# RWKV-7 attention with hash-routed experts on one core: the loads of tiles 4 to 7, the third round of decays, the order of transposes and scores, and the turnings

## The chip, the cores and the metric

The kernel runs on one core of one Trainium2 chip. The metric is the time of one execution on the device in microseconds (us); a lower one is better. Several engines work side by side, each through its own queue, strictly in order: TensorE (PE, matmuls and transposes), VectorE (DVE), ScalarE (ACT), GpSimd (POOL) and SyncE (SP, which here only issues transfers). ACT and POOL can issue transfers as well. An instruction that waits holds everything behind it on its engine.

## The reference, cut to what matters

```python
B, H, S, D = (4, 8, 768, 40)          # r, k, v, w, a, b: (B, H, S, D), float32
for t in range(S):
    y[:, :, t] = einsum('bhd,bhde->bhe', r_t, state)
    Sa = einsum('bhde,bhe->bhd', state, a_t)
    state = state * w_t[:, :, None, :] - einsum('bhd,bhe->bhde', Sa, b_t)
    state = state + einsum('bhd,bhe->bhde', v_t, k_t)
x = y.transpose(0, 2, 1, 3).reshape(3072, 320)
expert = token_ids * 2654435761 % 8
for e in range(8):                     # w1[e]: 320 x 1024, w2[e]: 1024 x 320
    out[expert == e] = relu(x[expert == e] @ w1[e]) @ w2[e]
```

The first half is a recurrence over 768 steps with a 40 x 40 state for each of 32 heads; the second half sends each of 3072 tokens through one of eight experts.

## The kernel before, in words

**Tiles.** The recurrence is done in chunks of 64 steps. A tile is one chunk of one of two pairs of batches, so there are 24 tiles; tile u belongs to chunk u // 2. Four tiles (two chunks) share a *round* of decays, so there are six rounds, 0 to 5. Four tiles also share one *inversion* of small triangular blocks on DVE.

**Decays** (`decays`, one call for each round). The decays w are loaded (`pb`), clamped (L270), multiplied up as prefixes and suffixes (L275, L292), and closed by `own` (L280, L282), an `exchange` of block ends on PE (`ex_ps`), `ends` (ACT L297 to L302, DVE L299) and `recip` (L306, L307). `spread_all` multiplies the results through (L311; on GpSimd from round 1 on). Then p and q are turned so that time lies on partitions: by DVE (`turned`, L315), with three copies for the second half of q (L333 to L335, by SP except in round 0); round 1 instead writes both to DRAM and reads them back (`store` L340, L323, L329), all on SP's queue. `t_turn` holds the ticks of `turn_p` and `turn_q`.

**Preparing a tile** (`tile_a`). a goes into `at`, b and k into `z` (a slot of `z_all`; four transfers at L420, each 64 rows of eight runs of 160 bytes). GpSimd (DVE for tiles 0 to 3) multiplies `at` by p and `z` by q (L427). PE transposes them (`t_ps` L490, `z_ps` L458), ACT copies the result out (`at_t` L444, `z_t` or `cv` L459). PE forms the scores `a_ps` (L218, reading `z_t` and `at_t`); ACT copies parts of them out (`no`, `pk`), and `mk` is their masked copy: by DVE (L486), or for tiles 4 to 7 by ACT (L483) and then GpSimd (L484).

**Inversion** (`group_i`). DVE turns `pk` (`nb`, L512), does 31 pairs of products and sums (L521, L524), and turns the result twice (`ut` L532, `ug` L533).

**The recurrence** (`tile_m`, `tile_s`, `tile_b`). It follows the preparation at a distance of eight tiles: `x_ps` and `u_ps` (from `ut`, `ug`), `r_ps` in two parts, `c_ps`, `rc_ps`, whose masked copy is `mr` (DVE L650), `nc_ps`, `s_ps`, whose scaled copy `sc` (DVE L676) is the new state, `y_ps` and its copy `xs` (L694), which GpSimd's queue stores into `x_rows`. The routing of tokens (`routing`) is laid between, a step every half tick; its first step loads the tokens (`tok`, L741) and reads them on DVE (`eid`, L748).

**Order.** Every piece of work is registered with a *tick*; the pieces are sorted by tick and emitted in that order, and this is the order in each engine's queue. Tile u's preparation lies around tick u (closer for tiles 4 to 7), its recurrence around tick u + 8. PSUM buffers for `z_ps`, `t_ps`, `a_ps` and others alternate between two.

**Experts.** After the recurrence, rows of `x_rows` are gathered by expert, go through two matrix products (`up_ps`, `dn_ps`) and are scattered to the output.

Of the kernel before, what the change touches and what calls it, by code (L numbers as in the profile page):

```python
# [18 lines left out]
def kernel(  # L19
# [13 lines left out]
    nc = tc.nc  # L33
# [8 lines left out]
    NG = B // 2  # L42
# [87 lines left out]
    def at_tick(tick, step=None, order=0):  # L130
        if step is not None:
            tick += STEPS.index(step) / len(STEPS)

        def add(f):
            plan.append((round(tick, 4), order, len(plan), f))
            return f
        return add
# [11 lines left out]
    at_r = ring("at", 3, [P, HP, P], gaps, 3)  # L149
    NZ = LAG + 2  # L150
    z_all = hold.tile([P, NZ, 2, HP, P], F32, name="z_all")
    for lo, hi, when in ((0, 4, -9.0), (4, NZ, -3.0)):
        @at_tick(when)
        def _(lo=lo, hi=hi):
            nc.gpsimd.memset(z_all[:, lo:hi].rearrange("p i b hp (two x) -> p (i b hp two) x", two=2)[:, :, D:C], 0.0)

    def z_r(u):
        return z_all[:, u % NZ]
# [17 lines left out]
    for be in range(2):  # L176
        rows = slice(be * C, (be + 1) * C)
# [49 lines left out]
    def per_head(t):  # L227

        return t.rearrange("t hp (two x) -> t (hp two) x", two=2)[:, :, 0:D]
# [156 lines left out]
    def tile_a(u):  # L386

        n, g = divmod(u, NG)
        ri, rn = divmod(n, RN)
        x = tiles[u]  # L390

        early = u < 2 * NG
        second = 2 * NG <= u < 4 * NG
        eng = (nc.sync, nc.scalar)[u % 2] if early else nc.sync
        if early:
            t_in = t_inz = -8.9 + 0.01 * u
            t_mul = -6.0 + 0.01 * u
            t_mulz = -6.1 + 0.01 * u if u < 2 else t_mul - 0.005
            t_z, t_at, t_a = u - 0.3, (-0.15, 0.5, 0.95, 1.0)[u], u + 0.9 if u < 3 else u + 0.4
        elif second:  # L400
            base = 4 + 0.7 * (u - 4)
            t_in = t_inz = (0.55, 0.97, 0.2, 1.05)[u - 4]
            t_mul = base - 0.5
            t_mulz = t_mul
            t_z, t_at, t_a = base - 0.3, base - 0.15, base + 0.4
        else:
            t_in, t_inz, t_mul, t_mulz = u - 2.3, u - 1.42, u - 0.9, u - 0.6
            t_z, t_at, t_a = (u - i + STEPS.index(n) / len(STEPS) for i, n in ((0, "z"), (1, "at_t"), (0, "a")))

        @at_tick(t_in)  # L410
        def _():
            x["z"] = z_r(u)
            x["at"] = r1_r(u // GRP) if u in (3, 7) else at_r(u)
            load(eng, x["at"][:], a, g, n * C)

        @at_tick(t_inz)
        def _():
            for be in range(2):
                for src, rows in ((b, half(be)), (k, half(1 - be))):
                    eng.dma_start(per_head(x["z"][rows, be]),  # L420
                                  src[batch(g, be), :, n * C:(n + 1) * C, :].rearrange("h t e -> t h e"))

        cols = slice((rn * NG + g) * DM, (rn * NG + g + 1) * DM)

        def times(eng, t, by):
            t = per_head(t)
            eng.tensor_tensor(t, t, by.rearrange("p (h e) -> p h e", e=D), op=OP.mult)  # L427

        @at_tick(t_mul)
        def _():  # L430
            times(nc.vector if early else nc.gpsimd, x["at"][:], rounds[ri]["p"][:, cols])

        @at_tick(t_mulz)
        def _():
            for be in range(2):
                times(nc.vector if early else nc.gpsimd, x["z"][:, be], rounds[ri]["q"][:, be, cols])

        @at_tick(t_at)
        def _():
            x["at_t"] = t = at_t_r(u)  # L440
            p = psum("t_ps")
            for be in range(2):
                turn(p, 0, x["at"][half(be)], be, half(be))
            nc.scalar.copy(t[:].rearrange("p b hp t -> p b (hp t)"), p[:, :, 0:HP * C])  # L444

        @at_tick(t_z)
        def _():
            if early and u % 2:
                z_t = cv[:].rearrange("p a b t -> p (a b t)").rearrange("p (b hp i t) -> p b hp i t", b=2, hp=HP, i=2)
            else:  # L450
                z_t = work.tile([P, 2, HP, 2, C], F32, tag="z_t", name="z_t", bufs=1)[:]
            x["z_t"] = z_t
            p = psum("z_ps")
            for i in range(2):
                for be in range(2):
                    for hp in range(HP):
                        c0 = (be * HP + hp) * C
                        nc.tensor.transpose(p[:, i, c0:c0 + C], x["z"][half(i), be, hp, :], ident[half(i), half(i)])  # L458
            nc.scalar.copy(z_t.rearrange("p b hp i t -> p i (b hp) t"), p[:].rearrange("p i (h t) -> p i h t", t=C))  # L459

        @at_tick(t_a)
        def _():
            gi, ti = divmod(u, GRP)
            p = psum("a_ps")
            for kind in range(2):
                for hp, par, be in quarters():
                    i = be ^ kind
                    c0 = (kind * HP + hp) * C
                    mm(p[half(i), par, c0:c0 + C], x["z_t"][half(par), be, hp, i, :], x["at_t"][half(par), be, hp, :])
            if ti == 0:  # L470
                groups[gi]["pk"] = work.tile([P, GRP, 2, HP, BLK], F32, tag="pk", name="pk", bufs=1)
            pk = groups[gi]["pk"][:, ti]
            pb, pa = (p[:, :, kind * HP * C:(kind + 1) * HP * C].rearrange("p two (hp t) -> p two hp t", hp=HP) for kind in range(2))
            x["no"] = no = work.tile([P, 2, HP, BLK], F32, tag="no", name="no", bufs=LAG)
            nc.scalar.copy(no[:], pb[..., BLK:])
            nc.scalar.copy(pk, pb[..., 0:BLK])
            for be in range(2):
                low = slice(be * C + BLK, (be + 1) * C)
                nc.scalar.copy(pk[low], pb[low, :, :, BLK:])
            x["mk"] = mk = work.tile([P, 2, HP, C], F32, tag="mk", name="mk", bufs=LAG)  # L480
            mask = after[:].unsqueeze(1).unsqueeze(1).to_broadcast([P, 2, HP, C])
            if second:
                nc.scalar.copy(mk[:], pa)  # L483
                nc.gpsimd.tensor_tensor(mk[:], mk[:], mask, op=OP.mult)  # L484
            else:
                nc.vector.tensor_tensor(mk[:], pa, mask, op=OP.mult)  # L486
# [82 lines left out]
    def tile_s(u, t0):  # L569

        n, g = divmod(u, NG)
        ri, rn = divmod(n, RN)
        x = tiles[u]

        @at_tick(0.4 + 0.2 * u if u < 2 else t0 - 2.0)
        def _():
            x["r"], x["x"] = r_r(u), x_all[:, u % 3]
            load(nc.sync, x["r"][:], r, g, n * C)
            for be in range(2):
                nc.sync.dma_start(per_head(x["x"][half(1 - be), be]),  # L580
                                  v[batch(g, be), :, n * C:(n + 1) * C, :].rearrange("h t e -> t h e"))

        @at_tick(t0 - 0.3)
        def _():
            x["py"] = py = work.tile([P, DM], F32, tag="py", name="py", bufs=1)
            cols = slice((rn * NG + g) * H, (rn * NG + g + 1) * H)
            nc.gpsimd.dma_start(py[:], p_dram[ri][:, cols].rearrange("t c e -> t (c e)"))

        @at_tick(t0 - 1, "rv")
        def _():  # L590
            x["rt"] = t = work.tile([P, 2, HP, C], F32, tag="rt", name="rt", bufs=1)
            p = psum("t_ps")
            for be in range(2):
                turn(p, 0, x["r"][half(be)], 1 - be, half(be))
            for be in range(2):
                turn(p, HP * C, x["x"][half(1 - be), be], be, half(1 - be))
            nc.scalar.copy(t[:].rearrange("p b hp t -> p b (hp t)"), p[:, :, 0:HP * C])
            nc.scalar.copy(cv[:, :, 2:4].rearrange("p hp b t -> p b hp t"),
                           p[:, :, HP * C:].rearrange("p b (hp t) -> p b hp t", hp=HP))
# [110 lines left out]

    t_a = STEPS.index("a") / len(STEPS)
    decays(0, -9.0, -8.0, (-7.9, -7.6), -7.7, -7.5, -6.9, -7.2, None)
    decays(1, -8.5, 0.1, (0.15, 1.85), 1.88, 2.75, 3.02, 2.85, (3.1, 3.15))
    decays(2, -5.5, 0.45, (0.5, 2.5), 3.38, 3.41, 4.0, 3.5, (6.45, 6.46))
    for ri in range(3, NR):
        t = ri * RN * NG
        decays(ri, t - 5.8, t - 5.3, (t - 5.2, t - 3.9), t - 3.75, t - 3.17, t - 2.17, t - 3.1, (t - 1.57, t - 1.44))
    for u in range(NU):
        tile_a(u)
        tile_s(u, u + LAG)  # L720
# [370 lines left out]
```

## Time and profile before

Three timed runs gave 754.02, 762.84 and 766.64 us, median 762.84. The profile comes from a separate execution.

| what | value |
|---|---|
| profiled execution, time | 748.57 us |
| its span (first to last instruction) | 746.8 us |
| mean granted TensorE clock | 0.892 |
| busy: PE, DVE, ACT, POOL | 622.0, 354.7, 272.1, 242.4 us |
| PE busy in 0 to 100 us | 34.1 us |
| PE busy in 140 to 460 us | 300.5 us |
| tile 0's recurrence starts on PE (its first `x_ps`) | 101.39 us |
| transfers | 76.74 MB, mean 103 GB/s |

In the rows below, a time on the left is the start in us from the beginning of the span, and the next number is how long it took. "x16" means 16 instructions merged into one row. "[0.71 <-ACT at_t L444]" says that the engine was idle for 0.71 us before this and what ended the wait. SPq is SP's queue, issuing a transfer. The page's strips cut the span into 40 slices and give the busy share, or the granted clock, in tenths.

### The profile page before, as it was taken

Reading aid. Unit: us, or ns where it says so; the run is one execution under the profiler, and the core shown is the slowest. Engines: PE = TensorE matmul, PEld = TensorE weight load, DVE = VectorE, ACT = ScalarE, POOL = GpSimd, SP = SyncE. Lnnn points to the kernel's source line nnn. Section 1 sums busy time; section 2 is a strip of 40 time slices with the busy share of each in tenths; the row PEclk is TensorE's granted clock in tenths of the full one; section 3 lists DMA queues with packets and bytes.
Section 4 is the critical chain, followed back from the end, with each engine's and each line's share of the span. In section 5 each row is a group of like instructions: output and inputs, shape, how many; then the busy total and the mean of one; then the engine's idle time right before and its main releaser. Section 6 shows DMA issues by size and latency. Waiting matters only on the chain.

```text
span 746.8 us, 24358 instructions
## 1 busy us (share of the span) xinstructions
PE 622.0 (83%) x10686; PEld 467.0 (63%) x10686; DVE 354.7 (47%) x721; ACT 272.1 (36%) x611; POOL 242.4 (32%) x311
## 2 busy tenths in 40 slices
PE   0450588999899989999998994498999999999994
PEld 0340577888787777878887884255556465565652
DVE  6889564897866768576495211115311111102100
ACT  1550454467556646756754461111010101111010
POOL 4060754525473664453321011503022121310101
PEclk9995556599789989999998898599899999999997
DMA  9479253356647644663343223967413253120000
GB/s 164 104 114 183 46 117 61 60 116 142 110 69 152 103 73 106 129 112 57 53 61 62 50 57 117 354 223 252 146 43 92 93 182 101 52 89 9 27 3 29
DMA packets 164158, 76.74 MB, mean 103 GB/s; under 512 B 143247, under 2 KB 155536, under 8 KB 164049
## 3 DMA queue, kind: packets, MB, share of 16 engines
q1 hardware_dynamic: 151632, 57.76, 35.5%
q0 software_dynamic: 5952, 16.08, 7.1%
q10 hardware_dynamic: 6464, 1.31, 1.1%
q8 instruction: 85, 1.39, 0.8%
q14 instruction: 25, 0.20, 0.1%
HBM read 58.69 MB, written 12.82 MB: 96 GB/s over the span
## 4 chain that ended last, share of the span: by engine, by line
PE 48%; issue 19%; DVE 12%; ACT 7%; POOL 5%; DMA 4%; SPq 3%; POOLq 0%; DVEq 0%; ACTq 0%
PE dn_ps L926 7%; PE up_ps L906 5%; PE r_ps L218 5%; PE rc_ps L218 4%; PE s_ps L218 4%; PE u_ps L218 3%; PE t_ps L490 3%; PE y_ps L218 3%; PE a_ps L218 3%; POOL xg L885 3%; PE z_ps L458 2%; PE c_ps L218 2%; PE sd_ps L706 2%; PE nc_ps L659 2%; PE up_ps L902 2%
## 5 line engine op out<-in xcount | busy, mean ns | idle before, releaser
L926 PE MATMUL dn_ps<-w,ht 128*128 128x320 f32 x384 | 104.9, 433 | 0.0
L906 PE MATMUL up_ps<-xt,w 128*128 128x416 f32 x256 | 97.6, 536 | 0.0
L926 PEld LDWEIGHTS dn_ps<-w,ht 128*128 128x128 f32 x384 | 72.8, 190 | 32.1 <-issue 1.9
L916 POOL DMA_INDIRECT out_dram<-o,idx_all x26 | 25.7, 989 | 194.5 <-ACT o L915 187.4
L697 POOL DMA_DIRECT2D x_rows<-xs x48 | 26.8, 562 | 163.8 <-DVE xs L694 120.5
L906 PEld LDWEIGHTS up_ps<-xt,w 128*128 128x128 f32 x256 | 49.2, 197 | 48.4 <-issue 48.4
L524 DVE TENSOR_TENSOR ub<-ub,outer 128x31 f32<-128x31 f32 (+15 forms) x186 | 65.0, 349 | 6.4
L521 DVE TENSOR_TENSOR outer<-ub,nb 128x31 f32<-128x31 f32 (+15 forms) x186 | 63.0, 339 | 7.4 <-ACT ub L506 2.8
L909 DVE TENSOR_SCALAR ht<-up_ps 128x416 f32<-128x416 f32 x32 | 18.9, 592 | 98.8 <-PE up_ps L906 98.8
L891 DVE COPY xt<-xg_ps 128x384 f32<-128x384 f32 x24 | 12.1, 552 | 101.8 <-PE xg_ps L890 101.8
L458 PE MATMUL z_ps<-ident,z_all 64*128 64x64 f32 x384 | 31.2, 270 | 34.8 <-POOL z_all L427 24.6
L650 DVE TENSOR_TENSOR mr<-rc_ps,after 128x1024 f32<-128x1024 f32 x24 | 29.3, 1222 | 60.3 <-PE rc_ps L218 60.3
L458 PEld LDWEIGHTS z_ps<-ident,z_all 64*128 64x128 f32 x384 | 27.0, 174 | 37.6 <-POOL z_all L427 25.6
L915 ACT COPY o<-dn_ps 128x320 f32<-128x320 f32 x24 | 10.2, 425 | 101.6 <-PE dn_ps L926 101.6
L427 POOL TENSOR_TENSOR z_all<-z_all,qt 128x320 f32<-128x320 f32 x40 | 33.9, 864 | 33.9 <-DMA z_all<-in_k_dram 14.7
L911 ACT ACTIVATE ht<-up_ps 128x416 f32<-128x416 f32 x32 | 16.0, 515 | 68.1 <-PE up_ps L906 68.1
L218 PE MATMUL rc_ps<-rt,cv 64*64 64x64 f32 x1536 | 37.0, 240 | 3.9 <-issue 2.5
L679 ACT COPY st<-sc 40x320 f32<-40x320 f32 x44 | 20.1, 457 | 55.1 <-DVE sc L676 54.9
L902 PE MATMUL up_ps<-xt,w 64*128 64x416 f32 x128 | 30.8, 568 | 8.0 <-DVE xt L891 3.2
L218 PEld LDWEIGHTS rc_ps<-rt,cv 64*64 64x64 f32 x1536 | 30.0, 148 | 10.6 <-issue 7.1
L459 ACT COPY z_t<-z_ps 128x1024 f32<-128x1024 f32 x22 | 22.3, 1013 | 39.2 <-PE z_ps L458 39.1
L885 POOL DMA_INDIRECT xg<-x_rows,src_all x26 | 27.2, 1046 | 28.7 <-PE xg_ps L890 16.1
(186 smaller groups left out, 1185.3 us busy)
## 6 DMA issues: line engine op xcount, KB each, us to landing
w<-in_moe_w_dram SPq DMA_DIRECT2D x8, 1280.0 KB
w<-in_moe_w_dram SPq DMA_DIRECT2D x8, 1024.0 KB
r<-in_r_dram SPq DMA_DIRECT2D x48, 80.0 KB
x_all<-in_v_dram SPq DMA_DIRECT2D x48, 80.0 KB
qt<-qt SPq DMA_DIRECT2D x12, 320.0 KB
py<-p_rows POOLq DMA_DIRECT2D x24, 160.0 KB, 3.8
x_rows<-xs POOLq DMA_DIRECT2D x48, 80.0 KB, 3.5
wt<-in_w_dram SPq DMA_DIRECT2D x6, 640.0 KB
```

The source lines that it names most:

```text
L218: nc.tensor.matmul(out_, lhsT=lhsT, rhs=rhs, start=start, stop=stop, skip_group_check=True)
L427: eng.tensor_tensor(t, t, by.rearrange("p (h e) -> p h e", e=D), op=OP.mult)
L458: nc.tensor.transpose(p[:, i, c0:c0 + C], x["z"][half(i), be, hp, :], ident[half(i), half(i)])
L521: nc.vector.tensor_tensor(tv, ub[:, 0:j + 1, j:j + 1].to_broadcast([P, j + 1, m]), nb[:, j, j + 1:].unsqueeze(1).to_broadcast([P, j + 1, m ...
L524: nc.vector.tensor_tensor(o, o, tv, op=OP.add)
L650: nc.vector.tensor_tensor(t[:].rearrange("p two h t -> p (two h) t"), p[:].rearrange("p two (h t) -> p (two h) t", t=C), after[:].unsqueez ...
L697: nc.gpsimd.dma_start(x_rows[r0:r0 + C, :], xs[half(be)])
L885: nc.gpsimd.indirect_dma_start(out=xg[:, 0:DM], out_offset=None, in_=x_rows[:], in_offset=bass.IndirectOffsetOnAxis(ap=idx, axis=0))
L902: nc.tensor.matmul(banks[-1][:], lhsT=w1[rows, w:w + P], rhs=xt[rows, 2, 0:n], start=True, stop=False)
L906: nc.tensor.matmul(p[:], lhsT=w1[:, c * F + f * P:c * F + (f + 1) * P], rhs=xt[:, c, 0:n], start=False, stop=(c == 1))
L916: st = nc.gpsimd.indirect_dma_start(out=out[:], out_offset=bass.IndirectOffsetOnAxis(ap=idx, axis=0), in_=o[:], in_offset=None, bounds_che ...
L926: nc.tensor.matmul(p[:], lhsT=ht[:, f, j * P:(j + 1) * P], rhs=w2[:, f, :], start=(f == 0), stop=(f == FP - 1))
```

## The change

It consists of six edits.

- b and k of tiles 4 to 7 are loaded from GpSimd's queue at tick -8.6 instead of SP's queue at ticks 0.2 to 1.05; `z_all` is zeroed in three pieces instead of two, so that the piece of tiles 4 to 7 is done before. r and v of tiles 0 and 1 are loaded at tick 5.0 and 5.2 instead of 0.4 and 0.6.
- Round 1's exchange, ends and spread come at 2.95 to 2.97 instead of 2.75 to 2.85, behind the scores of tile 2, and the step that forms `pend` at 3.6 instead of 3.02.
- Round 2's steps from `own` on come at 6.41 to 7.85 instead of 3.38 to 6.46. `own` then stands behind the first inversion on DVE, the exchange behind `a_ps` of tile 7 and `x_ps` of tile 0 on PE, and the spread behind all of GpSimd's work for tiles 4 to 7.
- For tiles 4 to 7 the scores come 0.05 tick later, behind the next tile's `z_ps`; the odd ones of these tiles use `cv` for their transposed z, as tiles 1 and 3 did.
- From tile 8 on, `z` is multiplied ahead of `at` (ticks u - 0.75 and u - 0.66 instead of u - 0.6 and u - 0.9).
- In rounds 3 to 5 q is turned at t - 1.72 and p at t - 0.72, instead of p at t - 1.57 and q at t - 1.44, where t is the round's first tile.

```diff
-    for lo, hi, when in ((0, 4, -9.0), (4, NZ, -3.0)):
+    for lo, hi, when in ((0, 4, -9.0), (4, 8, -8.7), (8, NZ, -3.0)):
...
         elif second:
             base = 4 + 0.7 * (u - 4)
-            t_in = t_inz = (0.55, 0.97, 0.2, 1.05)[u - 4]
+            t_in, t_inz = (0.55, 0.97, 0.2, 1.05)[u - 4], -8.6 + 0.01 * u
             t_mul = base - 0.5
             t_mulz = t_mul
-            t_z, t_at, t_a = base - 0.3, base - 0.15, base + 0.4
+            t_z, t_at, t_a = base - 0.3, base - 0.15, base + 0.45
         else:
-            t_in, t_inz, t_mul, t_mulz = u - 2.3, u - 1.42, u - 0.9, u - 0.6
+            t_in, t_inz, t_mul, t_mulz = u - 2.3, u - 1.42, u - 0.66, u - 0.75
...
                 for src, rows in ((b, half(be)), (k, half(1 - be))):
-                    eng.dma_start(per_head(x["z"][rows, be]),
+                    (nc.gpsimd if second else eng).dma_start(per_head(x["z"][rows, be]),
...
         @at_tick(t_z)
         def _():
-            if early and u % 2:
+            if u < 4 * NG and u % 2:
                 z_t = cv[:].rearrange("p a b t -> p (a b t)").rearrange("p (b hp i t) -> p b hp i t", b=2, hp=HP, i=2)
...
-        @at_tick(0.4 + 0.2 * u if u < 2 else t0 - 2.0)
+        @at_tick(5.0 + 0.2 * u if u < 2 else t0 - 2.0)
...
     decays(0, -9.0, -8.0, (-7.9, -7.6), -7.7, -7.5, -6.9, -7.2, None)
-    decays(1, -8.5, 0.1, (0.15, 1.85), 1.88, 2.75, 3.02, 2.85, (3.1, 3.15))
-    decays(2, -5.5, 0.45, (0.5, 2.5), 3.38, 3.41, 4.0, 3.5, (6.45, 6.46))
+    decays(1, -8.5, 0.1, (0.15, 1.85), 1.88, 2.95, 3.6, 2.97, (3.1, 3.15))
+    decays(2, -5.5, 0.45, (0.5, 2.5), 6.41, 6.65, 7.85, 6.7, (6.96, 7.0))
     for ri in range(3, NR):
         t = ri * RN * NG
-        decays(ri, t - 5.8, t - 5.3, (t - 5.2, t - 3.9), t - 3.75, t - 3.17, t - 2.17, t - 3.1, (t - 1.57, t - 1.44))
+        decays(ri, t - 5.8, t - 5.3, (t - 5.2, t - 3.9), t - 3.75, t - 3.17, t - 2.17, t - 3.1, (t - 0.72, t - 1.72))
```

The arguments of `decays` are the round and the ticks of load, clamp, chain (from, to), own, exchange, `pend`, spread and the two turnings.

More of the change, by code (lines that the diff above doesn't have):

```diff
@@ L411, in _ @@
         def _():
-            x["z"] = z_r(u)
             x["at"] = r1_r(u // GRP) if u in (3, 7) else at_r(u)
@@ L417, in _ @@
         def _():
+            x["z"] = z_r(u)
             for be in range(2):
                 for src, rows in ((b, half(be)), (k, half(1 - be))):
-                    eng.dma_start(per_head(x["z"][rows, be]),
+                    (nc.gpsimd if second else eng).dma_start(per_head(x["z"][rows, be]),
                                   src[batch(g, be), :, n * C:(n + 1) * C, :].rearrange("h t e -> t h e"))
```

## The prediction

> **What bounds the kernel now.** I read the page first, for the stages. PE is busy for 83% of the span, but in slices 1 to 7 (each 18.7 us) its clock is often 5 tenths and its busy share low. PE work runs without large gaps only from about 130 us on.
>
> ```profile
> PE 622.0 (83%) x10686; PEld 467.0 (63%) x10686; DVE 354.7 (47%) x721; ACT 272.1 (36%) x611; POOL 242.4 (32%) x311
> PE   0450588999899989999998994498999999999994
> PEclk9995556599789989999998898599899999999997
> DMA  9479253356647644663343223967413253120000
> ```
>
> So the first 130 us are bound by hand-overs between engines, and most edits lie there. The chain of work that ended last, in order of time, says which. It runs through SP's queue of z loads, the round trip of round 1's decays through DRAM, GpSimd's spread of round 2's decays, the four a_ps, and later the token load.
>
> ```profile
> 54.94 0.64 SPq L420
> 55.64 0.45 issue
> 56.09 0.33 SPq L340
> ...
> 62.26 4.59 DMA q_rows<-qb
> 66.86 0.59 SPq L329
> 67.49 8.17 DMA qt<-q_rows
> ...
> 77.45 2.86 POOL pb L311
> 80.31 2.86 POOL qb L311
> ...
> 118.16 2.22 DMA tok<-in_moe_token_ids_dram
> ```
>
> The timeline, engine by engine, shows where round 2's decays ran: turned on DVE at 94.67 and 97.28, copied by SP until after 105.33, used by GpSimd for tile 8 at 107.45 (at) and 110.35 (z). PE started tile 8's turning at 108.49 without waiting and tile 0's r_ps at 109.12.
>
> ```profile
> 94.67 2.75 DVE L315 STREAM_TRANSPOSE pt<-pb 128x1280 f32<-128x1280 f32 x1 [8.51 <-POOL r L427]
> 97.28 2.69 DVE L315 STREAM_TRANSPOSE qt<-qb 128x1280 f32<-128x1280 f32 x1
> 99.48 1.98 PE L218 MATMUL a_ps<-at_t,z_t 64*64 64x64 f32 x64 [0.71 <-ACT at_t L444]
> 105.33 0.46 SPq L335 DMA_DIRECT2D qt<-qt  x1
> 107.45 0.86 POOL L427 TENSOR_TENSOR at<-at,pt 128x320 f32<-128x320 f32 x1
> 108.49 0.70 PE L490 MATMUL t_ps<-ident,at 64*128 64x64 f32 x8
> 110.35 0.86 POOL L427 TENSOR_TENSOR z_all<-z_all,qt 128x320 f32<-128x320 f32 x1 [0.36 <-DMA z_all<-in_k_dram]
> ```
>
> From 140 to 460 us the waits of PE sum to 19 us, none over 2.0: little to win there.
>
> **The change, part by part.** The order of instructions on each engine is written out by the ticks, so it can be followed by hand.
>
> *1. Round 1's exchange goes behind a_ps of tile 2.* a_ps(2) ran at 45.55 to 47.54. ACT's copies of it end at 49.03 and DVE's mk, now ahead of ends, at 49.75. Then ends 0.32, reciprocal 1.15, sign 0.24 give 51.6 for GpSimd's spread, against 47.59: 4.0 later, so p is spread at 54.5 and q at 57.4.
>
> *2. SP no longer issues the z loads of tiles 4 to 7, nor r and x of tiles 0 and 1, before the stores.* It stood in them until 55.58. Now p's stores start with the spread p at 54.5 instead of 56.09. From that start to q's landing took 66.86 - 56.09 = 10.8, the reload to 75.66 another 8.8. Tile 4's z can be multiplied at 74.1 instead of 75.7: 1.6 won of the 6 that the queue held. GpSimd's 5.75 of round 2's spread between tiles 4 and 5 go away too. The inversion starts at 53.8 instead of 56.89 and ends at 83, where nothing waits for it.
>
> *3. z's transposes ahead of the scores before.* PE now does z(u+1) before a_ps(u). But GpSimd multiplies z(u+1) only after mk(u-1), and this waits for ACT's copy of mk(u-1), about 2.1 after a_ps(u-1) ends. So one turn of the loop is: a_ps 2.0, ACT 2.1, GpSimd mk 1.25, at 0.83, z 1.65, rest of z_ps 1.0: 8.8 us, against 5.54 between a_ps at 93.94 and 99.48. a_ps(4) starts at 74.1 + 4.2 (two z, one at) + 1.0 = 79.3, a_ps(5) at 88.1, a_ps(6) at 96.9. a_ps(7) has no z before it: 2.0 + 2.1 + 0.65 later, 101.65, ending at 103.65 against 101.47. What parts 1 and 2 win is lost here: 2.2 later.
>
> *4. Round 2's decays behind the first inversion.* Its exchange stands on PE behind a_ps(7) and x_ps(0), so at 104.7 instead of 54.3. ACT first ends its copies of a_ps(7) and xi, 106.45; ends 0.3; DVE 0.32 + 1.15 + 0.24: 108.5. GpSimd's spreads 2.9 + 2.87: 114.3. DVE turns q, 2.7: 117.0. The copies between halves took from 99.97 to at most 110.35 (tile 8's z began then, but waited for its own load) and at least to 105.8 + 2 (L335 cannot land at once); I take 9.3, nearer the upper row: 126.3. Behind this wait in GpSimd's queue stand z(8) 1.7, one link of round 3's chain 0.5 and, since t_mul is now behind t_mulz, at(8) 0.86: 129.4. PE's queue holds t_ps(8) ahead of tile 0's r_ps, so with 0.7 r_ps begins at 130.1 instead of 109.12: **21.0 late**. Tile 0's rows, rc, s and y stand behind it.
>
> Some is given back. The mr of tile 0 waited in DVE's queue behind the token work, and that for a load behind r(2) and x(2) in SP's queue, 8.2 after PE had turned tile 0's r and x at 112.2. That turning is now at 133.1; SP is idle then: r 1.3, x 1.64, landing 2.3 give 138.4, and the 4.0 from eid to mr stay: mr at 142.4 against 124.4. Net of parts 1 to 4: **+18.0**, with about 2 either way for the copies. A clamp of round 3 now stands between DVE's sign and its turns; if GpSimd's spreads hold it as they held a row at 50.52 (2.98 instead of 0.32), 3.5 more: upper bound only.
>
> *5. Sixteen loads on GpSimd's queue in the first 20 us.* No row has such a load (512 runs of 160 B). GpSimd's cost: the nearest rows are stores of 64 rows, 0.56, and loads of 128 rows, 0.58; the slope gives 0.69, in proportion to 64 rows 4.5 would be the upper end. I take 0.69: 11 us in GpSimd's idle stretch from 9.94 to 32.35, with 5 of memsets behind, so it is covered. On the transfers: the 16 carry 1.31 MB, 8.0 us at the 164 GB/s of the first 20 us, where the DMA share is 0.98. ACT issues its last loads at 14.85, paced by landings, and only then its table load and the copies that release DVE's ends at 16.67. Everything after hangs on that. If the new loads use only gaps: 0; if they all go ahead: 8; with equal thirds from 5.6 on, 4.6. Taking the new wait for eight landings on GpSimd into account I take **+4**. DVE's clamp at 7.13 to 10.62 can end 2.7 sooner, since GpSimd's memsets that stood beside it (the same clamp takes 0.8 at 31.47) now come later; but ACT's copies end last, so this wins nothing.
>
> The row for the shares is that full DMA slice; it cannot show who goes first. [...]
>
> *6. The turnings of rounds 3 to 5.* q is now turned right behind mr, ahead of ut, ug and sc; p one tile later. At 159.9 DVE did ut, ug, then sc at 163.41, and PE's next r_ps waited for ACT behind it (0.9). At 227.93 and 292.47 sc is likewise what x_ps waited for. 2.7 more ahead of sc costs up to 2.9 for each of three rounds; nothing if x_ps and the copies cover it. I take 2 each: **+6**. Turning q in its old place delayed no row that PE waits for, so nothing comes back.
>
> Sum: 18 + 4 + 6 = 28. On the profiled execution, 748.6 us (span 746.8), this gives 776.6. The median of the runs shown is 762.84, 14.3 above it; on that footing the forecast is 762.8 + 28, about **790.5**.
>
> **The rivals.** *A: the tail of round 2 is hidden (not slower).* If its q copies landed before about 105, tile 8's z and at would be done by 108 as before. Then only gains would be left: 1.6 from part 2 and up to 5.75 of GpSimd's spread, about 7, less 6 in part 6: 762. For it: in before the same copies had 2 us of slack. Against: ex would have to run at 84, behind the inversion, while it stands behind a_ps(7). It decides from whether a_ps(7) ends before 85.
>
> *B: half of it is absorbed.* Part 4 stays, but the loads cost 0, the turnings 0 and the copies land 1.5 sooner: +16.5, 779. This is my low end.
>
> *C: GpSimd pays by runs.* At 4.5 a load, 16 take 72 us, and the memset that round 1's first product waits for moves from 32.35 to about 82: +50 on top, 840. For it: the runs are eight times the rows of a store. Against: twice the rows cost only 0.02.
>
> **How the numbers follow.** Forecast with B as its lower part: 0.84; A 0.10; C 0.06. About 2% (15 us) is what a measurement of this kernel can tell from no change. Bounds: low 18 - 2 + 0 + 0 = +16, less 10 for a part of A and for the scatter of the runs (754 to 767): 769. High 18 + 2 + 3.5 + 8 + 8.7 = +40, with 6 of scatter: 809. Faster by over 2% needs A and a gain in the rounds: 0.04. Within 2%: A's rest and the edge of B: 0.14. Slower: 0.82.
>
> **What would show it.** Right: the L315 of q at about 117 to 121, PE waiting some 20 us at t_ps(8) for GpSimd, 8.8 between the a_ps of tiles 4 to 6, ends of round 0 near 21. Wrong: r_ps of tile 0 before 115, or GpSimd's loads taking over 2 us each.

## The result and the profile after

| | before | after |
|---|---|---|
| timed side by side, median (lowest to highest) | 758.43 us (751.71 to 766.64) | 796.51 us (794.56 to 802.07) |
| profiled execution, time and span | 748.57 and 746.8 us | 797.2 and 795.4 us |
| mean granted TensorE clock in it | 0.892 | 0.865 |
| first `mr` (tile 0) | 124.40 us | 148.98 us |
| from first to last `mr` (tile 23) | 332.8 us | 357.7 us |
| from last `mr` to the end of the span | 289.6 us | 288.7 us |

The changed kernel is slower by the ratio 1.054 [1.042, 1.067]. (Ratios here leave out executions more than 1.5% above the fastest of the same kernel, so they are not quite the quotients of the medians.) The medians differ by 38 us. In the later comparisons before's medians were 746 to 754; the changed kernel was not timed again beside them, so the cost lies between 38 and some 50 us. The profiled executions differ by 48.6: 24.6 lost ahead of the first `mr`, 24.9 between the first and the last, -0.9 behind.

The page after, to be laid beside the four lines of before:

```profile
PE 630.0 (79%) x10686; PEld 476.4 (60%) x10686; DVE 352.6 (44%) x721; ACT 272.6 (34%) x611; POOL 255.2 (32%) x328
PE   0350552998979989898989899459899999999991
PEclk9995555687899598868999999869999999999996
DMA  9719405337436543635423332497632162220000
```

A slice is now 19.9 us. PE's 2 in slice 7 (119 to 139 us) is the hole ahead of tile 8's turning; before, PE was at 8 and 9 by then. The second thing stands in the clock strip. From slice 9 to 24 it reads 8789959886899999, with eight nines; before it had eleven nines in those slices. PE has the same 10686 instructions as before and needs 8 us more for them.

The timeline of the startup, the rows that answer to those of before (tile 8's turning at 108.49, q turned at 97.28):

```profile
107.19 1.98 PE L218 MATMUL a_ps<-at_t,cv 64*64 64x64 f32 x64 [2.00 <-ACT at_t L444]
110.10 0.28 PE L218 MATMUL ex_ps<-own,ident 128*32 128x40 f32 x1
112.15 0.20 ACT L298 COPY qb<-ex_ps 128x40 f32<-128x40 f32 x1
112.43 0.32 DVE L299 TENSOR_TENSOR ends<-own,ex_ps 128x160 f32<-128x160 f32 x1 [23.77 <-ACT qb L298]
114.30 2.89 POOL L311 TENSOR_TENSOR pb<-pb,own 128x1280 f32<-128x1280 f32 x1 [1.69 <-DVE own L307]
114.35 3.52 DVE L270 TENSOR_SCALAR qb<-pb 128x1280 f32<-128x1280 f32 x1
117.15 3.50 POOL L311 TENSOR_TENSOR qb<-qb,ends 128x1280 f32<-128x1280 f32 x1
...
120.68 2.70 DVE L315 STREAM_TRANSPOSE qt<-qb 128x1280 f32<-128x1280 f32 x1 [0.21 <-POOL qb L311]
...
128.59 0.46 SPq L335 DMA_DIRECT2D qt<-qt  x1
132.01 1.67 POOL L427 TENSOR_TENSOR z_all<-z_all,qt 128x320 f32<-128x320 f32 x2 [8.18 <-DMA qt<-qt]
134.12 0.86 POOL L427 TENSOR_TENSOR at<-at,pt 128x320 f32<-128x320 f32 x1
135.03 0.70 PE L490 MATMUL t_ps<-ident,at 64*128 64x64 f32 x8 [18.77 <-POOL at L427]
...
141.33 0.62 SPq L741 DMA_DIRECT2D tok<-in_moe_token_ids_dram  x1
145.25 0.18 DVE L748 TENSOR_SCALAR eid<-tok 128x24 int32<-128x24 int32 x1 [16.37 <-DMA tok<-in_moe_token_ids_dram]
148.98 1.22 DVE L650 TENSOR_TENSOR mr<-rc_ps,after 128x1024 f32<-128x1024 f32 x1
```

This is the chain that the prediction wrote down, read from top to bottom. Round 2's exchange (`ex_ps`) stands on PE behind `a_ps` of tile 7, and ACT's copy of it ends DVE's wait of 23.77 us for `ends`; the inversion's last turning had ended at 87.8. GpSimd's spread and DVE's clamp of round 3 start at the same time. Then come q's turn, the copies between the halves, `z`, and behind it `at`. PE stood still for 18.77 us.

The loss in the steady part is a different matter. The first two fences are VectorE's and then TensorE's timeline at tile 2. The third is the table by stretch: from:to, length, PE busy (instructions), granted clock, DMA share and GB/s. Its stretches are 3.41 us long.

```profile
182.40 1.21 DVE L650 TENSOR_TENSOR mr<-rc_ps,after 128x1024 f32<-128x1024 f32 x1
183.53 2.69 DVE L315 STREAM_TRANSPOSE qt<-qb 128x1280 f32<-128x1280 f32 x1
186.12 1.88 DVE L532 STREAM_TRANSPOSE ut<-ub 128x1024 f32<-128x1024 f32 x1
187.86 1.85 DVE L533 STREAM_TRANSPOSE ug<-ub 128x1024 f32<-128x1024 f32 x1
189.57 0.46 DVE L676 TENSOR_TENSOR sc<-s_ps,pend 128x320 f32<-128x320 f32 x1
```

```profile
185.80 1.08 PE L218 MATMUL y_ps<-z_all,mr 128*64 128x40 f32 x32
190.09 0.69 PE L218 MATMUL x_ps<-ut,no 32*32 32x32 f32 x32 [3.20 <-DVE sc L676]
```

```profile
184.04:187.45 3.41, 2.84 (x117) 1.00 0.42 108
187.45:190.86 3.41, 0.78 (x34) 1.00 0.88 186
190.86:194.28 3.42, 2.68 (x24) 0.50 0.55 113
194.28:197.69 3.41, 3.41 (x58) 0.50 0.88 168
197.69:201.10 3.41, 3.41 (x77) 0.50 0.58 111
201.10:204.52 3.42, 3.42 (x71) 0.50 0.31 48
204.52:207.93 3.41, 3.41 (x106) 1.00 0.02 5
```

q's turning (2.69) pushes `sc` back, and TensorE waits 3.20 at `x_ps`. That much was predicted. What comes next was not: with TensorE at work again, its clock stands at 0.50 for four stretches, 13.7 us in all. Matmuls take longer there: the 16 of `r_ps` take 1.34 us at 193.24, against 0.77 one tile earlier, at 174.05. Tile 2 to tile 3 takes 21.9 us from `mr` to `mr` instead of 15.0. The same happens at tile 6 (22.0 instead of 15.6) and tile 10 (21.9 instead of 15.0). The three places make 20.2 of the 24.9; the other 4.7 were not followed further.

### The profile page after: what moved, and what is told of

Same layout as the page of the kernel before. It is cut to its first block, busy times and chain, and to the rows that moved or that the text cites. A ratio compares the mean times of both kernels' runs of the same rounds, so it can differ in the third digit from the quotient of the medians.

```text
span 795.4 us, 24340 instructions
## 1 busy us (share of the span) xinstructions
PE 630.0 (79%) x10686; PEld 476.4 (60%) x10686; DVE 352.6 (44%) x721; ACT 272.6 (34%) x611; POOL 255.2 (32%) x328
## 4 chain that ended last, share of the span: by engine, by line
PE 58%; DVE 15%; issue 8%; DMA 7%; ACT 5%; POOL 3%; SPq 1%; ACTq 0%; POOLq 0%; DVEq 0%
PE dn_ps L926 11%; PE up_ps L906 9%; PE r_ps L218 5%; PE y_ps L218 3%; PE rc_ps L218 3%; PE a_ps L218 3%; PE s_ps L218 3%; PE t_ps L490 3%; PE u_ps L218 3%; PE up_ps L902 3%; PE sd_ps L706 2%; DVE outer L521 2%; PE z_ps L458 2%; DVE ub L524 2%; PE c_ps L218 2%
## 5 line engine op out<-in xcount | busy, mean ns | idle before, releaser
L906 PE MATMUL up_ps<-xt,w 128*128 128x416 f32 x256 | 93.7, 519 | 0.0
L906 PEld LDWEIGHTS up_ps<-xt,w 128*128 128x128 f32 x256 | 47.3, 190 | 45.8 <-issue 45.8
L679 ACT COPY st<-sc 40x320 f32<-40x320 f32 x44 | 20.1, 457 | 67.3 <-DVE sc L676 67.0
L427 POOL TENSOR_TENSOR z_all<-z_all,qt 128x320 f32<-128x320 f32 x40 | 34.1, 870 | 22.3 <-DMA qt<-qt 8.2
L218 PE MATMUL a_ps<-at_t,z_t 64*64 64x64 f32 x1280 | 29.0, 252 | 10.4 <-DVE mr L650 6.5
L902 PE MATMUL up_ps<-xt,w 64*128 64x416 f32 x128 | 29.1, 561 | 7.1 <-DVE xt L891 3.2
```

What stands on the lines that cost most here:

```text
L218: nc.tensor.matmul(out_, lhsT=lhsT, rhs=rhs, start=start, stop=stop, skip_group_check=True)
L902: nc.tensor.matmul(banks[-1][:], lhsT=w1[rows, w:w + P], rhs=xt[rows, 2, 0:n], start=True, stop=False)
L906: nc.tensor.matmul(p[:], lhsT=w1[:, c * F + f * P:c * F + (f + 1) * P], rhs=xt[:, c, 0:n], start=False, stop=(c == 1))
```

## The experiments

The changed kernel was not timed again beside these runs, and before's median moved by up to 12 us between the comparisons (746.42 to 758.43). Differences of medians to the changed kernel can therefore be off by as much; the rows and the `mr` times of the profiles carry the argument.

Theory S says: a stall of TensorE is followed by a stretch at half clock, which costs more than the stall. Its rivals are P (the stall alone, as predicted) and C (the clock just happened to be lower).

**1. The old turnings in the changed kernel.**

```diff
-        decays(ri, ..., (t - 0.72, t - 1.72))
+        decays(ri, ..., (t - 1.57, t - 1.44))
```

> The changed kernel with the turnings of rounds 3 to 5 back behind sc (two ticks). Theory S (a stall and then a slow clock): each of the three turnings makes TensorE wait 2 to 3 us at x_ps, and the granted clock then stands at about half speed for some 10 us, which costs another 4 to 5; so from the first mr to the last it should be about 20 us shorter (337 instead of 357.7 in the profile), and the execution about 20 us shorter, near 776. Rival P (the plain stall, as predicted): only the stalls themselves come back, 6 us, near 790. Rival C (the clock merely stood lower in that execution, whatever the kernel): no change within the scatter, and the half-speed stretches stay as long.

Measured: median 783.05 us (778.31 to 793.82), 13.5 less than the changed kernel; 349.5 from first to last `mr`. Neither S's numbers nor P's fit. The waits of PE between 140 and 500 us say why (total, times, longest):

```profile
PE t_ps L490 <- POOL at L427: 7.2, 2, 3.7
PE x_ps L218 <- DVE sc L676: 2.2, 2, 2.0
```

The stalls at `x_ps` of tiles 2, 6 and 10 are gone (the 2.0 left are tile 18's, as before), but the undoing was only half: `at` is still multiplied behind `z`, and `z` waits for q, which is again turned late. So `t_ps` waited 3.47 at 206.5 and 3.72 at 277.1, and a half-clock stretch came with each.

**2. More work for TensorE.**

```diff
+            for again in range(2 if u in (2, 6, 10) else 1):   # around the whole y product
```

> The changed kernel, with the y product of tiles 2, 6 and 10 worked out twice in a row (32 more matrix products of 64x80 and 64x40 in each, about 1.9 us, just ahead of TensorE's wait for sc); the output is the same. Work is only added. Theory S: TensorE now stands still for only about 1.3, 0.5 and 0.2 us at those three places, the clock does not fall there, and the kernel gets about 4 to 5 us faster for each, 10 to 15 in all. Rival P: the added work lies inside the stalls, so no change (0 to +1). Rival C: no change.

Measured: 786.91 us (785.53 to 787.73), 9.6 less than the changed kernel, whose four executions were all at 794.56 or more; 346.6 from first to last `mr` instead of 357.7. Adding matmuls made the kernel faster, which P and C cannot give. In its profile `x_ps` of tile 6 follows without a wait and at full clock; in the changed kernel it waited 2.32 and took 1.33:

```profile
265.12 0.69 PE L218 MATMUL x_ps<-ut,no 32*32 32x32 f32 x32
```

Tile 6 to 7 took 17.9 us instead of 22.0, tile 10 to 11 17.5 instead of 21.9. This is not chance: in the five profiles that keep the new turnings without added work (the changed kernel and runs 3, 5, 7 and 12) both took 21.9 to 22.3 every time. Tile 2 to 3 stayed at 22.0: there 0.90 of the wait was left, a stall of 1.47 us (`r_ps`, at 194.1) came right behind it, and the half clock all the same. So S holds, at two of the three places.

**3. The new turnings alone, in the kernel before.**

```diff
-            t_in, t_inz, t_mul, t_mulz = u - 2.3, u - 1.42, u - 0.9, u - 0.6
+            t_in, t_inz, t_mul, t_mulz = u - 2.3, u - 1.42, u - 0.66, u - 0.75
...
-        decays(ri, ..., (t - 1.57, t - 1.44))
+        decays(ri, ..., (t - 0.72, t - 1.72))
```

> The kernel before with nothing but the turnings of rounds 3 to 5 (and the two multiplications of tiles 8 and on) at their new ticks. Theory S: about +20 us on the kernel before, with the first mr where it was (124) and the last some 20 later. Rival P: +6. Rival C: 0.

Measured: 776.32 us (771.09 to 778.63) beside 753.75, ratio 1.040 [1.027, 1.053]. From first to last `mr` 352.9 instead of 332.8, that is +20.1, with 21.9 at each of tiles 2, 6 and 10. The other 3.5 lie at the start (first `mr` 127.92): `at` of tile 8 now waits behind its `z` there too, 5.93 us at `t_ps`. S fits.

**4. The loads alone, in the kernel before.**

```diff
-            t_in = t_inz = (0.55, 0.97, 0.2, 1.05)[u - 4]
+            t_in, t_inz = (0.55, 0.97, 0.2, 1.05)[u - 4], -8.6 + 0.01 * u
...
-                    eng.dma_start(per_head(x["z"][rows, be]),
+                    (nc.gpsimd if second else eng).dma_start(per_head(x["z"][rows, be]),
```

The zeroing of `z_all` in three pieces belongs to it too.

> The kernel before with nothing but the z loads of tiles 4 to 7 moved from SyncE to GpSimd at the start. If what the loads do is delay ACT's loads by 5 us, ends of round 0 come at 21.7 instead of 16.7, but SyncE is free of these loads when round 1's stores are due: spread p ends at 50.5 + 5 = 55.5 and the stores start there instead of at 56.1. Theory L (the two cancel): 0, between -2 and +1, with tile 0's r_ps at 107 to 110. Rival D (the delay is handed on whole): +5, with r_ps of tile 0 at 114.

Measured: 753.58 us beside 753.75, ratio 1.006 [0.996, 1.016]. `ends` of round 0 came at 21.94 (5.3 later), the stores at 55.77 instead of 56.09, tile 4's `z` at 75.74 instead of 75.78, `r_ps` of tile 0 at 107.18 instead of 107.22. The delay and the free queue cancel, as theory L has it.

**5. `at` ahead of `z` for tiles 8 to 11, in the changed kernel.**

```diff
+            if u < 12:
+                t_mul, t_mulz = u - 0.9, u - 0.6
```

> The changed kernel, in which GpSimd multiplies at of tiles 8 to 11 ahead of their z again, as before (t_mul u - 0.9, t_mulz u - 0.6 for these four). Theory O (tile 8's at waits in GpSimd's queue behind z, and z for the copies of q between the halves, while at itself needs only p, turned at 120.5): t_ps of tile 8 then starts near 121.5 instead of 135, the first mr comes some 10 to 13 us sooner (136 to 139 instead of 149), and the median falls from 796.5 to about 784 to 787. Rival K (tile 0 hangs on the copies of q by another way too, since tile 8's z is turned on TensorE in tile 0's steps): 0 to -4, the wait turning up at z_ps. In both the steady part stays as long, about 358 from first to last mr.

Measured: 787.4 us (784.68 to 797.09). `t_ps` of tile 8 started at 123.06 instead of 135.03, yet the first `mr` came at 143.85, only 5.1 sooner, and 1.4 of that was already there at ends of round 0 (20.23). O was right on the wait, and K on its worth, though not through `z_ps`. The next thing late is SyncE's queue in that kernel (whose lines are numbered two higher from L408 on):

```profile
128.06 0.46 SPq L335 DMA_DIRECT2D qt<-qt  x1
128.57 0.65 SPq L422 DMA_DIRECT2D z_all<-in_b_dram  x1
...
135.24 1.32 SPq L582 DMA_DIRECT2D x_all<-in_v_dram  x2
136.61 0.62 SPq L743 DMA_DIRECT2D tok<-in_moe_token_ids_dram  x1
```

The last copy of q waits there 4.5 us for the first two, with the loads of the next tiles and the token load behind it. `eid` follows at 139.44, `mr` 4.4 later.

**6. Part 6 undone whole.** Run 1 and the old `t_mul` and `t_mulz` together, in the changed kernel.

> The changed kernel with part 6 undone whole: the turnings back behind sc, and at ahead of z for every tile from 8 on. Theory O with S (stall, then a slow clock): the waits of 3.5 and 3.7 us for GpSimd at t_ps, which the run with the old turnings alone had at 206.5 and 277.1, are gone, the part between first and last mr is near the 333 us of before, the first mr comes at 136 to 139; in all about 25 us less than the 783 of that run less its own excess: 762 to 768. Rival: the startup keeps its whole loss of 24.6 and only the steady part recovers, about 777.

Measured: 778.55 us (776.94 to 780.07), 18 less than the changed kernel. The two waits at `t_ps` are gone, tiles 2 and 10 take 14.9 and 15.1. First to last `mr` is 339.2, first `mr` 145.64. The rival's number came out. The startup keeps 21.2 of its 24.6, as in run 5 because of SyncE's queue, where the last copy of q is issued at 130.12 and the token load at 138.37.

**7. Round 2 back at its old ticks, in the changed kernel.**

```diff
-    decays(2, -5.5, 0.45, (0.5, 2.5), 6.41, 6.65, 7.85, 6.7, (6.96, 7.0))
+    decays(2, -5.5, 0.45, (0.5, 2.5), 3.38, 3.41, 4.0, 3.5, (6.45, 6.46))
```

> The changed kernel with the decays of round 2 back at their old ticks (exchange 3.38, ends 3.41, spread 3.5, turnings 6.45 and 6.46), all else as changed. As the prediction has it (part 4 carries the startup loss), tile 8's at is ready near 118 instead of 134, r_ps of tile 0 starts near 119, the first mr comes 14 to 18 us sooner than 149, and the median falls to 779 to 783. Rival Z (the loop of z ahead of the scores carries it, with GpSimd's spread of 5.75 us now inside that loop): only 0 to -6, with a_ps of tile 7 at 113 instead of 107.

Here `pend` of round 1 is formed after round 2's ends have taken the place of round 1's, so the state in round 1 is scaled by round 2's factors. So it computes something else; the order of the instructions is what was wanted. Measured: 788.22 us (777.01 to 795.11), first `mr` at 139.1, 9.9 sooner; `a_ps` of tile 7 at 114.45 instead of 107.19. It lies between the two theories. Run 12 repeats it with round 1 as before.

**8 and 9. Two additions to the kernel before.** Run 8 is run 4 with the loads at tick -2.9 + 0.01 u, behind GpSimd's memsets. Run 9 adds matmuls:

```diff
+            for again in range(2 if u == 18 else 1):          # around the whole y product
+                for more in range(3 if u == 4 else 1):        # around its first half
```

> The kernel before with the z loads of tiles 4 to 7 on GpSimd, as in the run with these loads alone, but put behind GpSimd's own memsets (about 10 to 21 us instead of 5 to 17). Theory: they meet fewer of ACT's loads, whose last is issued at 14.85 without them. ends of round 0 then comes at 18 to 19.5 (16.7 before, 21.9 with the early loads), the spread of p ends near 53, its stores start there instead of at 56.1, tile 4's z is multiplied at 73 instead of 75.8, and the first mr comes 2 to 3 us sooner than 124.4. In the median 2 to 3 us at most. Rival: the transfers cost ACT the same wherever they lie: ends at 21.7, 0 in all.

> The kernel before with TensorE work added where it stands still: in tile 4 the first half of the y product three times (1.5 us more, ahead of the wait of 1.67 us for mr), in tile 18 the whole y product twice (1.9 us more, ahead of the wait of 1.97 us for sc). The output is the same. Theory S (such a stall is followed by half clock for 10 to 15 us): the half-speed stretches at 195 to 209 and 403 to 417 do not come, 5 to 7 us gained for each, so 742 to 746 beside a median of 754. Rival P (a stall costs only itself): 0 to +1.

Run 8: `ends` of round 0 at 16.70, not delayed at all (18.53 in run 11, with the same loads), the stores at 50.52, the first `mr` at 118.08, 6.3 sooner than before and more than expected. The median, 748.74 beside 749.95, ratio 0.999 [0.995, 1.004], shows none of it. In its profile the part from first to last `mr` took 342.5 instead of 332.8, with 19 windows of 3.4 us at half clock where before had 15. Whether that always takes the gain back is open.

Run 9 is a miss: 752.55 us (748.77 to 755.06) beside 746.42, ratio 1.012 [1.003, 1.020]. The two stalls were filled, yet tile 4 to 5 took 16.9 us as before. Tile 18 to 19 took 13.2 instead of 17.5; but runs 4 and 8, where nothing was added, have 13.2 there too. Stalls of 1.47, 1.48 and 1.65 us at 167.3, 201.7 and 335.4 were followed by half clock in its profile. So S was not shown here. The last section counts what followed stalls of this length in all the profiles.

**10 and 11. A version to beat both.** The half-clock stretch at tile 18 follows a wait of `x_ps` for `sc`, and `sc` stands behind `ut` and `ug` on VectorE. `ug` is not needed until the next tile's `u_ps`.

```diff
             nc.vector.transpose(ut[:].rearrange("p g s -> p s g"), ub[:])
-            nc.vector.transpose(ug[:].rearrange("p g t -> p t g"), ub[:].rearrange("p s t -> p t s"))
+        @at_tick(t2 + 0.1 if gi else t2, order=9)
+        def _():
+            ...
+            nc.vector.transpose(ug[:].rearrange("p g t -> p t g"), ub[:].rearrange("p s t -> p t s"))
```

> The kernel before with one instruction moved on VectorE: the transposition ug of each group stands behind sc instead of ahead of it (ut stays). ug is needed only by u_ps of the next tile, sc by x_ps at once. Theory S: the stall of 2 us at x_ps of tile 18, which every profile so far shows, goes, and with it a possible half-speed stretch behind it; the sc of tiles 2, 6, 10 and 14 comes 1.9 us sooner as well. From first to last mr 324 to 330 instead of 332.8, median 3 to 8 us less. Rival: the stall only moves to u_ps or to the copies behind it, 0 within 2 us.

> The kernel before with both: the z loads of tiles 4 to 7 on GpSimd behind its memsets, and ug behind sc. If the two theories hold: first mr near 122, 324 to 330 from there to the last, median 5 to 10 us less than before. If their rivals hold: 0.

Measured: run 10 741.79 us beside 749.95, ratio 0.991 [0.987, 0.995]; run 11 743.61, ratio 0.994 [0.991, 0.999]. Both beat the kernel before, by less than 1%. VectorE's timeline at tile 18 in run 11, and TensorE's row that waited 1.97 us before (in this kernel `ut`, `sc` and `ug` are L531, L680 and L537):

```profile
396.54 1.97 DVE L531 STREAM_TRANSPOSE ut<-ub 128x1024 f32<-128x1024 f32 x1
398.37 0.46 DVE L680 TENSOR_TENSOR sc<-s_ps,pend 128x320 f32<-128x320 f32 x1
398.76 1.91 DVE L537 STREAM_TRANSPOSE ug<-ub 128x1024 f32<-128x1024 f32 x1
398.89 0.69 PE L218 MATMUL x_ps<-ut,no 32*32 32x32 f32 x32 [0.25 <-DVE sc L680]
```

Tile 18 to 19 takes 11.4 us (11.5 in run 10) instead of 17.5. Not all of these 6 us are the edit's doing: with the wait in place it took 13.2 to 17.5 in eleven profiles, 15.9 on average. Run 11's profile has 328.3 from first to last `mr`, as expected; run 10's, of its slowest execution (750.6), has 335.4, with half clock in tiles 6 and 7 behind another stall. The loads added nothing to `ug`'s gain that the medians show.

**12. Parts 1 and 4 undone.** Both lines of `decays` as before, all else as changed.

> The changed kernel with both lines of decays as before (round 1 and round 2), all else as changed: parts 1 and 4 undone. By the sum of the prediction (part 4 and part 1 carry the startup's 18, the loads 4 to 5): tile 0's r_ps near 114 to 116 and the first mr near 131, 18 sooner than 149, the steady part as long as in the changed kernel (358), median near 778. Rival Z: with GpSimd's spread of 5.75 us back inside the loop of z ahead of the scores, and tile 8's at still behind z, r_ps of tile 0 comes at 120 to 123 and the first mr at 136 to 139, median 783 to 787.

Measured: 783.74 us (772.47 to 786.49). First `mr` at 133.7, 15.3 sooner than in the changed kernel, between the two theories. `a_ps` of tiles 4 to 7 at 86.17, 95.15, 104.13 and 108.74: the turn is 8.98 us, `a_ps` of tile 7 lies 9.3 us behind before (99.48), and so does the first `mr`. So parts 1 and 4 together hold 15.3 of the startup's 24.6, and what is left as changed 9.3. Tile 4's `z` came at 75.24, no later than before (75.78), so the loads do not make the 9.3; they arise between this `z` and `a_ps` of tile 7, in the z-ahead loop (with GpSimd's spread back in it).

## Why the prediction was right, and where it was not

The direction, the chain and most of the sizes held; the time fell inside the range. By its steps:

- *Parts 1 and 5.* Round 1's spread came at 56.52 instead of 47.59: 8.9, against 4.0 + 4. Most of the loads cost GpSimd 0.69 us each, as the slope had it, with 0.99 the longest, which ends rival C. ACT's table load moved from 14.85 to 20.05, +5.2.
- *The price of the loads.* `ends` of round 0 came at 20.23 to 23.29 in the eight profiles with these loads at their new tick, and at 16.67 to 17.62 in four without them (before and runs 3, 9 and 10): 5.2 later on average, nearer to the estimate by equal shares (4.6) than to the 8 of loads that all go ahead. GpSimd waited for a landing once among its sixteen loads, for 0.60 us ahead of the last, at 16.30.
- *Part 2.* Tile 4's `z` at 79.14 instead of 75.78: +3.4, against -1.6 + 4.
- *Part 3.* The scores of tiles 4, 5 and 6 at 84.64, 93.61 and 102.58: a turn of 8.97 against 8.8.
- *Part 4.* `r_ps` of tile 0 was 26.95 late, against 21.0 + 4. DVE began to turn q at 120.68 instead of at 114.3 + 4, that is 2.4 later. The 3.5 put down as an upper bound did not come: DVE's clamp took 3.52 beside GpSimd's spread, but q's turning then waited only 0.21, for the spread. This had begun at 114.30 instead of 108.5 + 4, mostly because `a_ps` of tile 7 came at 107.19 instead of 101.65 + 4, and it took 6.35 instead of 5.77. The copies took 8.6 from the end of that turn to `z`, against 9.3. The first `mr` was 24.6 late, against 18 + 4.
- *Part 6 is the term that failed.* "I take 2 each: +6." The stalls were 3.20, 2.32 and 2.30 us, so the mechanism was there and the waits nearly of the size. But the term was 20: run 3 has 20.1 for these edits alone from first to last `mr`, and run 2 shows at two of the three places that the rest is the clock. The prediction looked at the clock only in the startup.
- *The footing.* The sum of 28 was put on a median of 762.84. (762.8 + 28 is 790.8, not 790.5.) Later medians of before were 9 to 16 us lower, and the profiled execution 14. Between the profiled executions the change cost 48.6, 20 more than the sum; the high footing hid 14 of them. So it is luck that 790.5 against 796.5 is closer than the steps were.
- Rivals A and B: nothing was hidden, the loads did delay `ends` of round 0 by some 5 (which the free queue of SyncE gives back, by run 4), the turnings did not cost 0.
- *What was looked past.* Of the waits of PE from 140 to 460 us the prediction said "little to win there". Taking away the longest of them, and bringing `sc` forward at four more tiles, won 8 us in run 10.

## What to carry to other kernels

Price a new wait of the bottleneck engine with the clock, not only with its own length: three waits of 2 to 3 us cost 20 us here, and lifting one 2 us wait out of TensorE's way (one transposition of each inversion moved behind `sc`, which comes sooner at four other tiles as well) won 0.9% on the kernel before. Before moving work later, follow each queue it is moved past to the second instruction that is held: here the wait at `t_ps` hid a later one in SyncE's queue, and taking the first away gave back 5 us of 12.

## What the runs showed of the hardware

*Where the clock changed.* In the 14 profiles of this study, from 100 us to each one's last `mr`, the granted clock is 0.50 or 1.00, and it changes 186 times. Within each profile the changes lie whole multiples of 3.4133 us apart, to 0.01 us (37 of them make the 126.29 us at full clock from 277.66 in before); where they lie in the span differs from profile to profile. They cut TensorE's timeline into windows of that length. Of the windows at full clock, those in which TensorE stood still for under 0.6 us were followed by half clock 0 times in 906; from 0.6 to 1.2 us, 6 times in 114; from 1.2 to 1.6, 21 in 45; from 1.6 up, 57 in 61. So after 1.2 to 1.6 us of standstill in one window the half clock came about every other time, and one profile with such a stall settles nothing; after 1.6 us or more it came in 93% of the cases. What decides between them these runs do not show.

*How long it stays.* From the first `mr` on, the half clock lasted one to five windows, 3.4 to 17.1 us, in many cases with TensorE busy all the time (seven of the eleven such stretches of before and after); the twelve longer stretches (six or seven windows) all began with a window in which it stood still for 0.26 us or more. What decides the length these runs do not show.

*One stall, several prices.* The wait of `x_ps` for `sc` at tile 18 was 1.96 to 1.99 us long in eleven profiles. Tile 18 to 19 took 13.2 us in the two where no half clock followed, 14.6 in the three with one window of it, and 17.4 or 17.5 in the six with three or four.

*Scatter.* The 13 executions of before beside runs 1 to 4 ran from 737.56 us (mean clock 0.915) to 761.51 us (0.875), the shorter ones almost in the order of their clocks. What sets the mean clock of one execution of the same kernel these runs do not show.

*VectorE beside GpSimd.* The clamp L270 takes 0.8 to 1.1 us with no GpSimd instruction beside it, 3.50 beside GpSimd's memsets at 7.12 before, and 3.52 beside its spread at 114.35 after. In both, and in nine more rows like them in the other runs, it ended some 0.7 us after that GpSimd work (here at 10.62 and 117.87, after 9.94 and 117.19).
